# Sums and differences of mirrored samples ahead of the second transform stage, as 64 by 64 products, and a new plan for the front

## The chip, the cores and the metric

The kernel runs on one core of a Trainium2 chip. The metric is the device time of one execution in microseconds; the kernel before takes 508.01 us, the median of three runs (507.02 to 508.63). The engines are named as in the profile: PE (TensorE), DVE (VectorE), ACT (ScalarE), POOL (GpSimd), and SP, which here only issues DMAs. PE reads its operands from SBUF and writes PSUM.

## The reference

For a sequence of L = 2048 tokens with D = 512 channels, the output is a gated sum of two branches of the same input x:

```python
g = sigmoid((x * gate_w).sum(-1, keepdims=True))
K = einsum("dn,dnl,dn->dl", Cc, exp(dt * A * l), dB).real          # taps: 512 channels, 2048 long, 128 states
a = irfft(rfft(pad(x)) * rfft(pad(K)))[:L] + x * Dskip            # causal convolution along the sequence
b = gelu(x @ w1 + b1) @ w2 + b2                                   # dense branch, 512 -> 1792 -> 512
out = g * a + (1 - g) * b
```

## The kernel before, in words

The program has two parts. **The front** (`front`) does the whole dense branch but its last bits, makes the taps K, and runs the first transform stage of the signal and of the taps. **The tail** (`conv`) does the second stage of both transforms, their product, the two inverse stages, the gate and the output.

A transform of 2048 samples is split as 32 times 64. The first stage (`first_stage`, L438) multiplies 32-row slices by c1t, a 32 by 64 matrix (32 complex frequencies), and its result goes through DRAM (`tu_d` for the signal, `tk_d` for the taps) so that the 64 remaining samples of each of the 32 frequencies come to lie on partitions: 128 rows are 64 real and 64 imaginary parts. The second stage (`pair`, L1152, called from `taps` and `signal` in the tail) turns these 128 rows into 64 real and 64 imaginary results for each frequency: one product of all 128 rows by a 128 by 64 matrix for the real part, one by another for the imaginary part. Of the second matrix only the first is loaded (c2); `matrices` makes it from the loaded one by a swap of halves and a sign, on POOL for the first two groups of four frequencies, on ACT for the other six. A step s of the tail takes two frequencies: `product` multiplies the two spectra on DVE in six operations (L1174 to L1179), `inverse` (L1191) does the first inverse stage in 64 by 64 products, and `turn` sends the result through DRAM (`t_d`) to the final stage (L1316). PE's order within a step is signal(s+1), taps(s+2), inverse(s). Nine leftover products of the dense branch stand before the inverse of the last step and the others behind it (`rest`).

The order of all work in the front is set by a planner (`Plan`). Each piece of work has an engine, a cost, a due time and the buffers that it reads and writes; the planner lets each engine take the ready piece with the lowest due time, and the program is then written in that order, fixed for each engine. The due times come from some fifty numbers at the head of the file (T_0, K_0, U_0, D_S1 and so on). In the front each block of 256 tokens goes through `hidden` (L917 to L919: three float32r products for each 128 by 128 tile of w1), gelu on ACT, a subtraction on DVE (L947) and `output` (L962 to L964). The taps come in 16 groups: DVE builds powers (L532 to L535), magnitudes (L689) and rotations (L701 to L712), PE contracts them (`contract`, L726), DVE adds the skip term (L743), ACT copies the result to SBUF (L744, tile s), and after every second group a first stage runs; ACT copies its four results into `sk` (L752), and after four groups SP stores them to `tk_d` (L767).

POOL in the front only clears buffers (L678) and issues DMAs: the reloads of x (L848) and the additions into the output in DRAM (L992, L1006). The signal's slots lie in the order of `slot_q`, which puts mirrored samples q and 63 - q into slots 32 apart.

Of the kernel before, what the change touches and what calls it, by code (L numbers as in the profile page):

```python
# [17 lines left out]
P = 128  # L18
L = 2048
D = 512  # L20
# [12 lines left out]
NB = 2 * NSB  # L33
T_0 = 28.031
T_MLP = 402.005
K_0 = 34.529
T_KG = 347.257
U_0 = 23
U_GAP = 18
LAG = 13.166  # L40
TABLE = 30.571
D_KA = -21.02
D_KP = -70.174
D_S1 = -64.005
D_EV = -0.687
D_H = -44.182
D_LO = -26.872
PS = (2, 3, 1, 2)
N_ACC, N_H, N_PK, N_PU = PS
D_SP = -0.459  # L50
MEM = (6, 2, 3)
N_LD, N_HL, N_ST = MEM
D_XS = -150.061
D_G = 2.936
N_WARM = 13
T_EARLY, T_LOFT, T_DEN = 434.731, 499.385, 583.061
Y_K, Y_U = 40.448, 33.741
W_MLP = (-0.0424, -0.0295, 0.0137)
W_KG = (-0.0358, -0.0266, -0.0229)
W_U = (-0.0255, -0.1355, -0.0209)  # L60
D_MAG = -1.089
D_ROT = 0.621
D_CON = -2.254
D_PHA = 0.57
D_PRE = -1.138
D_XL = 26
D_COE = -4.808
D_OUT = -10.383
D_DTB = -996.723
D_D0A = -269.982  # L70
D_LAST = -1.103
N_REST = 3
D_KA0 = 35
D_DT = 5
D_PRM = -94
D_D0 = 0
D_WAVE0 = -333.922
D_COE0 = -195.511
D_SP1 = -346.272
D_G0 = 14  # L80
D_GW = 568.694
D_XS0 = 115.71
T_PRE = 23
W_CAST = (0, 1, 0, 0, 1, 0, 1, 0, 1, 1, 0, 1, 0, 0)
X_CAST = (1, 1, 1, 1)
D_X0, D_B2, D_B2A, D_DM = -480, 20, -11.213, -79.268
N_G = 9
# [44 lines left out]
def constants():  # L132
# [7 lines left out]
    p = np.arange(32)  # L140
    q = np.asarray(slot_q())
    k1 = np.arange(64)
# [3 lines left out]

    c1 = np.tile(np.stack([er, ei], 2).reshape(32, 64), (4, 1))

# [21 lines left out]

    f2 = np.zeros((32, 2, 64, 64))
    g2 = np.zeros((32, 64, 32, 2))
    for n, k in enumerate(ko):
        er, ei = om(4 * np.outer(q - 31.5, k + 32 * k1) + (q - 31.5)[:, None])
        f2[n, 0], f2[n, 1] = er, -ei
        a = 2.0 * np.pi * (k + 32 * k1 + 0.25) / L
        g2[n, :, :, 0] = np.cos(np.outer(a, m))
        g2[n, :, :, 1] = np.sin(np.outer(a, m))
        g2[n, :, 0, 1] = 1 - 2 * (k1 % 2)
# [131 lines left out]
def gated_mix(  # L311
# [33 lines left out]
    gate = cp.tile([P, 2, 16], F32, name="gate")  # L345
    c1t = cp.tile([P, 64], F32, name="c1t")

# [5 lines left out]
    def front(pool, psum, keep, attic, loft, den):  # L353
# [45 lines left out]
        ux = [rooms[0], *tiles(1, [P, D], "ux")]  # L399
        s1 = tiles(2, [P, D], "s1")  # L400

        xh, xlo = (
# [24 lines left out]

        def first_stage(xs, due, evac, ahead=2):

            q = (step[0] + ahead) % N_H  # L430
            banks = [(phs[q].rearrange("p a b -> p (a b)"), ("h", q)), (pks[0].rearrange("p g s -> p (g s)"), ("pk", 0))]
            banks += [(pus[k], ("pu", k)) for k in range(2)]

            def products():
                for r, (bank, _) in enumerate(banks):
                    rs = slice(32 * r, 32 * r + 32)
                    for m, (x, _) in enumerate(xs):
                        nc.tensor.matmul(bank[64 * m : 64 * m + 64], c1t[rs], x[rs], start=True, stop=True)  # L438
# [7 lines left out]
        def signal():  # L446
            for s in range(8):
                t = U_0 + 16 * U_GAP * warp(s / 8, W_U)
                yield t + Y_U
                xs = [(ux[m], ("ux", m)) for m in range(2)]  # L450
                for m in range(2):
                    move(256, lambda m=m, s=s: nc.sync.dma_start(ux[m], xl[2 * s + m]), t - 10, [], [("ux", m)])

                def evac(r, pp, key, s=s, t=t):
                    k = take("st", N_ST)
                    act(512, lambda: nc.scalar.copy(st[k], pp), t + D_EV, [key], [("st", k)])
                    for m in range(2):
                        move(
                            128, lambda m=m: nc.sync.dma_start(rows[:, 8 * s + 4 * m + r], st[k][64 * m : 64 * m + 64]),
                            t, [("st", k)], [("u_d", 8 * s + 4 * m + r)], out=True,  # L460
                        )

                first_stage(xs, t, evac)
            yield None
# [251 lines left out]
        def contract(u, c, k, t):  # L716
# [27 lines left out]
            act(512, lambda: nc.scalar.copy(xs, pks[q].rearrange("p s g -> p (s g)")), t + D_S1, [("pk", q)], [key])  # L744
            pair.append((xs, key))
            if c % 2 == 0:
# [11 lines left out]

            first_stage([pair.pop(0), pair.pop(0)], t, evac, 1 if g == 4 * NCH - 1 else 2)
            if c < NCH - 1:  # L760
# [349 lines left out]
    def conv(pool, ps, late, attic, loft, den):  # L1110
# [5 lines left out]
        ko = k0_order()  # L1116
        c4s, mats, t2s = {}, {}, {}

        def consts(m):
            cc = pool.tile([P, 384], F32, tag="cc", name=f"cc{m}", bufs=4)  # L1120
            nc.sync.dma_start(cc, c2[m])
            c4s[m] = cc

# [6 lines left out]

        def matrices(m):

            cc = c4s[m]
            f = cc[:, 0:256].rearrange("p (n k) -> p n k", n=4)
            f1 = pool.tile([P, 4, 64], F32, tag="f1", name=f"f1{m}", bufs=2)
            if m < 2:
                nc.gpsimd.tensor_scalar(f1[0:64], f[64:128], -1.0, None, ALU.mult)
                nc.gpsimd.tensor_copy(f1[64:128], f[0:64])
            else:
                nc.scalar.mul(f1[0:64], f[64:128], -1.0)  # L1140
                nc.scalar.copy(f1[64:128], f[0:64])
            mats[m] = (f, f1), cc[:, 256:384].rearrange("p (s k) -> p s k", s=2)

        fac, pus, prod, pas = {}, {}, {}, {}

        def pair(s, r, c, out):

            for i in range(2):
                n = 2 * s + i
                w = mats[n // 4][0][c][:, n % 4]  # L1150
                x = t2s[n] if r else us[n]
                nc.tensor.matmul(out[64 * i : 64 * i + 64], w, x, start=True, stop=True)  # L1152

        def taps(s):
            fac[s] = []
            for c in range(2):
                pk = ps.tile([P, D], F32, tag=f"pk{c}", name=f"p2k{s}{c}", bufs=1)
                pair(s, 1, c, pk)
                k = pool.tile([P, D], F32, tag=f"k{c}", name=f"k{s}{c}", bufs=2)
                nc.scalar.copy(k, pk)  # L1160
                fac[s].append(k)

        def signal(s):
            pus[s] = []
            for c in range(2):
                pu = ps.tile([P, D], F32, tag=f"pu{2 * (s % 2) + c}", name=f"p2u{s}{c}", bufs=1)
                pair(s, 0, c, pu)
                pus[s].append(pu)

# [87 lines left out]
        nc.sync.dma_start(g1t, g1.rearrange("p (b k) -> p b k", b=2))  # L1257
        matrices(0)
        matrices(1)
        taps(0)  # L1260
        signal(0)
        taps(1)
        for s in range(16):
# [22 lines left out]
            turn(s)  # L1286
            if s % 2 and s < 13:
                matrices(s // 2 + 2)
            if 7 <= s < 13:
# [132 lines left out]
```

## Time and profile before

| | |
|---|---|
| median of three runs | 508.01 us |
| profiled execution, span | 506.3 us (no other time of that execution is given; the median is 1.7 us above the span) |
| PE, DVE, ACT, POOL busy | 494.8, 429.0, 347.2, 53.5 us |
| front, to the first product of the second stage | 398.2 us |
| 16 steps of the tail, to the last inverse product | 398.2 to 476.6 us |
| leftover dense products, then final stage and output | 476.6 to 487.0, 487.0 to 506.3 us |

A float32 product shows as two records, so a row "x8" on L1152 or L1191 is four products. Durations of PE records overlap; the spacing of their starts, or the merged pieces of the chain of waits, tells what a product costs. In the views by stretch, each engine's busy time stands with its number of instructions in brackets, then the granted clock, the busy share of the 16 DMA engines and GB/s; the DMA share can pass 1.

### The profile page before, as it was taken

To read this page: it belongs to the slowest core of one execution; us is meant where nothing else is said; L and a number is where in the kernel's file an instruction comes from. 1 tells how busy PE (TensorE), PEld (TensorE's weight loads), DVE (VectorE), ACT (ScalarE), POOL (GpSimd) and SP (SyncE) were. 2 spreads that over 40 slices of the span, in tenths; PEclk is the share of its full clock that TensorE was granted. 3 is DMA by queue.
4 is the path that set the end of the run, shared out by engine and by line. 5 is a ranking of instruction groups with operands and counts; after the bars stand their busy time and mean duration, and the time that the engine had idled before them with its cause. 6 is when DMAs were issued, how large, how long until landed. Compare 5 with 4: busy or idle time off the path is not lost.

```text
span 506.3 us, 12185 instructions
## 1 busy us (share of the span) xinstructions
PE 494.8 (98%) x4798; PEld 380.3 (75%) x4798; DVE 429.0 (85%) x794; ACT 347.2 (69%) x625; POOL 53.5 (11%) x93
## 2 busy tenths in 40 slices
PE   7999999999999999999999999999999999999995
PEld 7886988998889889889789878989889722222551
DVE  6999999998999999999899989999921188877544
ACT  4898757699683889968487997657643445568513
POOL 1001010101002011011110012001010300020003
PEclk9999999999999999999999999999999999999998
DMA  8958896416788545889850276984588997999998
GB/s 288 381 178 235 298 296 219 84 65 200 182 239 222 156 147 126 262 187 238 201 128 2 84 167 156 208 266 104 189 208 180 282 390 266 336 374 382 320 321 312
DMA packets 82680, 112.32 MB, mean 222 GB/s; under 512 B 39644, under 2 KB 41184, under 8 KB 82080
## 3 DMA queue, kind: packets, MB, share of 16 engines
q1 hardware_dynamic: 74704, 87.06, 53.7%
q0 software_dynamic: 7264, 21.73, 18.3%
q10 hardware_dynamic: 656, 2.75, 1.7%
q8 instruction: 38, 0.62, 0.5%
q14 instruction: 18, 0.15, 0.1%
HBM read 61.71 MB, written 49.81 MB: 220 GB/s over the span
## 4 chain that ended last, share of the span: by engine, by line
PE 70%; DVE 13%; DMA 7%; ACT 4%; SPq 2%; issue 2%; DVEq 0%; ACTq 0%
PE pk L726 10%; PE acc L962 7%; PE ph L917 7%; PE ph L919 7%; PE ph L918 7%; PE acc L964 7%; PE acc L963 6%; PE p2u L1152 5%; PE p2k L1152 4%; PE pa L1191 3%; PE pb L1316 3%; DMA tk<-tk_d 2%; PE ph L438 2%; DVE y L689 2%; SPq L767 2%
## 5 line engine op out<-in xcount | busy, mean ns | idle before, releaser
L917 PE MATMUL ph<-xh,wh 128*128 128x256 f32 x448 | 127.7, 285 | 2.2 <-ACT wh L826 1.6
L919 PE MATMUL ph<-xh,wl 128*128 128x256 f32 x448 | 127.1, 284 | 0.4 <-DVE wl L828 0.4
L918 PE MATMUL ph<-xlo,wh 128*128 128x256 f32 x448 | 126.7, 283 | 0.0
L917 PEld LDWEIGHTS ph<-xh,wh 128*128 128x128 f32 x448 | 85.2, 190 | 9.5 <-issue 5.0
L918 PEld LDWEIGHTS ph<-xlo,wh 128*128 128x128 f32 x448 | 85.1, 190 | 1.8
L919 PEld LDWEIGHTS ph<-xh,wl 128*128 128x128 f32 x448 | 85.1, 190 | 1.0 <-DVE wl L828 1.0
L962 PE MATMUL acc<-wh,hh 128*128 128x512 f32 x206 | 83.2, 404 | 0.1
L964 PE MATMUL acc<-wh,hl 128*128 128x512 f32 x206 | 80.9, 393 | 0.5 <-DVE hl L947 0.5
L963 PE MATMUL acc<-wl,hh 128*128 128x512 f32 x206 | 80.9, 393 | 0.0
L934 ACT ACTIVATE ph<-ph,b1t 128x256 f32<-128x256 f32 x112 | 50.4, 450 | 43.6 <-PE ph L919 41.8
L726 PE MATMUL pk<-y,den 128*32 128x64 f32 x2048 | 61.4, 290 | 0.0
L726 PEld LDWEIGHTS pk<-y,den 128*32 128x32 f32 x2048 | 57.2, 136 | 3.5 <-issue 1.4
L962 PEld LDWEIGHTS acc<-wh,hh 128*128 128x128 f32 x206 | 38.7, 188 | 17.8 <-issue 7.4
L947 DVE TENSOR_TENSOR hl<-ph,hh 128x512 fp32r<-128x512 f32 (+1 forms) x62 | 38.4, 620 | 14.9 <-ACT hh L937 14.6
L689 DVE TENSOR_TENSOR y<-y,ea 128x64 f32<-128x64 f32 (+4 forms) x80 | 45.5, 569 | 2.1 <-ACT y L679 1.5
L964 PEld LDWEIGHTS acc<-wh,hl 128*128 128x128 f32 x206 | 38.7, 188 | 10.3 <-DVE hl L947 1.7
L963 PEld LDWEIGHTS acc<-wl,hh 128*128 128x128 f32 x206 | 38.7, 188 | 6.2
L937 ACT CAST hh<-ph 128x512 fp32r<-128x512 f32 (+1 forms) x62 | 33.0, 533 | 9.4 <-PE acc L963 6.2
L532 DVE TENSOR_TENSOR loft<-den,zz 128x256 f32<-128x256 f32 (+2 forms) x48 | 37.4, 779 | 0.7
L533 DVE TENSOR_TENSOR loft<-den,zz 128x256 f32<-128x256 f32 (+2 forms) x48 | 37.3, 777 | 0.0
L701 DVE TENSOR_TENSOR y<-y,loft 128x2048 f32<-128x2048 f32 x16 | 36.6, 2288 | 0.6 <-ACT loft L650 0.5
L1160 ACT COPY k<-p2k 128x512 f32<-128x512 f32 x32 | 18.5, 585 | 23.8 <-PE p2k L1152 8.0
(190 smaller groups left out, 876.0 us busy)
## 6 DMA issues: line engine op xcount, KB each, us to landing
tu_d<-attic SPq DMA_DIRECT2D x64, 128.0 KB, 3.9
tk_d<-sk SPq DMA_DIRECT2D x32, 256.0 KB, 5.3
t_d<-sa SPq DMA_DIRECT2D x32, 256.0 KB, 5.4
tk<-tk_d SPq DMA_DIRECT2D x24, 256.0 KB, 5.1
attic<-in_xt_dram SPq DMA_DIRECT2D x16, 256.0 KB, 5.1
xh_d<-xh SPq DMA_DIRECT2D x8, 512.0 KB, 5.0
xl_d<-xlo SPq DMA_DIRECT2D x8, 512.0 KB, 4.6
attic<-in_xs_dram SPq DMA_DIRECT2D x16, 256.0 KB, 4.9
```

Of the source, the lines that this page charges most:

```text
L532: vec(2 * m, lambda: vv.tensor_mul(t, a, br), due, [ka, *kb], [kt])
L689: nc.vector.tensor_mul(both(n, 64 - 3 * n, n), both(0, 64 - n, n), an)
L726: nc.tensor.matmul(pks[q][32 * j : 32 * j + 32, :, gg], x[:, r, :, ch], y[:, r, :, ch], start=(r == 0), stop=(r == 1), skip_group_check=True,)
L917: nc.tensor.matmul(p, h, xh[xk][:, d], start=(d == 0), stop=False)
L918: nc.tensor.matmul(p, h, xlo[xk][:, d], start=False, stop=False)
L919: nc.tensor.matmul(p, lo, xh[xk][:, d], start=False, stop=(d == 3))
L934: nc.scalar.activation(phs[q][:, n], phs[q][:, n], AF.Gelu_apprx_tanh, bias=b1t[:, f : f + 1])
L947: nc.vector.tensor_sub(lo, phs[q][:, 0:nf], hi.bitcast(F32))
L962: nc.tensor.matmul(a, h, wh[1][w], start=start, stop=False)
L963: nc.tensor.matmul(a, h, wl[1][w], start=False, stop=False)
L964: nc.tensor.matmul(a, l, wh[1][w], start=False, stop=(j == 3))
L1152: nc.tensor.matmul(out[64 * i : 64 * i + 64], w, x, start=True, stop=True)
```

## The change

For a real input at a real transform, the second stage on 64 slots needs only the sum of slots q and 63 - q for the cosine part and their difference for the sine part. The change makes these before the first stage. For the signal POOL subtracts and adds two loaded tiles of 512 columns (`ud`, `ux`), for which the two mirrored halves are now loaded together (`xl[s]` and `xl[s + 8]`); for the taps POOL subtracts and adds the halves of each copied contraction, 256 columns each (`sd`, and in place in `s1`). c1t gets a second matrix for the differences, so that what comes out of the first stage has 64 rows for the real result and 64 rows for the imaginary one. The taps' first stage works on half as many columns in twice as many products. In the tail each of the two results then needs 64 rows by a 64 by 64 matrix, and all matrices are loaded: `matrices` is gone. POOL's scratch for DMA descriptors is set to 8192 bytes, which makes room for the new tiles, and nearly all of the planner's numbers are others.

```diff
-T_0 = 28.031
+T_0 = 26.408
...
+D_UD = -20.4
...
+        def pool_op(n, fn, due, reads=(), writes=()):
+
+            return pl.add("GP", 0.18 + n / 470.0, fn, due, reads, writes)
...
-                    for m, (x, _) in enumerate(xs):
-                        nc.tensor.matmul(bank[64 * m : 64 * m + 64], c1t[rs], x[rs], start=True, stop=True)
-
-            mm(1.04, products, due + D_S1, [*(key for _, key in xs), "c1"], [key for _, key in banks], 0.5, 1.06, "f32")
+                    for m, parts in enumerate(xs):
+                        ms = slice(64 * m, 64 * m + 64)
+                        for x, at, sign in parts:
+                            c = c1t[rs, 64 * sign : 64 * sign + 64]
+                            nc.tensor.matmul(bank[ms, at], c, x[rs], start=True, stop=True)
+
+            mm(hold, products, due + D_S1, [*keys, "c1"], [key for _, key in banks], 0.5, 1.06, "f32")
...
-                    move(256, lambda m=m, s=s: nc.sync.dma_start(ux[m], xl[2 * s + m]), t - 10, [], [("ux", m)])
+                    move(256, lambda m=m, s=s: nc.sync.dma_start(ux[m], xl[s + 8 * m]), t - 10, [], [("ux", m)])
+                pool_op(512, lambda: nc.gpsimd.tensor_sub(ud, ux[0], ux[1]), t + D_UD, [("ux", 0), ("ux", 1)], ["ud"])
+                pool_op(512, lambda: nc.gpsimd.tensor_add(ux[0], ux[0], ux[1]), t + D_UD, [("ux", 1)], [("ux", 0)])
...
-            pair.append((xs, key))
+            low, high, df = xs[:, 0 : D // 2], xs[:, D // 2 : D], sd[c % 2]
+            pool_op(256, lambda: nc.gpsimd.tensor_sub(df, low, high), t + D_S1, [key], [("sd", c % 2)])
+            pool_op(256, lambda: nc.gpsimd.tensor_add(low, low, high), t + D_S1, [], [key])
+            pair.append([(low, slice(0, D // 2), 0), (df, slice(D // 2, D), 1)])
...
-        def matrices(m):
-
-            cc = c4s[m]
-            f = cc[:, 0:256].rearrange("p (n k) -> p n k", n=4)
-            f1 = pool.tile([P, 4, 64], F32, tag="f1", name=f"f1{m}", bufs=2)
-            if m < 2:
-                nc.gpsimd.tensor_scalar(f1[0:64], f[64:128], -1.0, None, ALU.mult)
-                nc.gpsimd.tensor_copy(f1[64:128], f[0:64])
-            else:
-                nc.scalar.mul(f1[0:64], f[64:128], -1.0)
-                nc.scalar.copy(f1[64:128], f[0:64])
...
-        def pair(s, r, c, out):
-
-            for i in range(2):
-                n = 2 * s + i
-                w = mats[n // 4][0][c][:, n % 4]
-                x = t2s[n] if r else us[n]
-                nc.tensor.matmul(out[64 * i : 64 * i + 64], w, x, start=True, stop=True)
+        def pair(s, r, outs):
+
+            for c in range(2):
+                rows = slice(64 * c, 64 * c + 64)
+                for i in range(2):
+                    n = 2 * s + i
+                    w = mats[n // 4][0][rows, n % 4]
+                    x = (t2s[n] if r else us[n])[rows]
+                    nc.tensor.matmul(outs[c][64 * i : 64 * i + 64], w, x, start=True, stop=True)
...
-    nc = bacc.Bacc("TRN2", target_bir_lowering=False, num_devices=1)
+    nc = bacc.Bacc("TRN2", target_bir_lowering=False, num_devices=1, dynamic_dma_scratch_size=8192)
```

Three places of the new order matter for what follows. The lines of the changed file stand lower by 10 to 20: L448 is the first stage, L462, L463, L759 and L760 are POOL's new operations, L691 clears, L867, L1011 and L1025 are POOL's DMAs, L786 the store of the taps, L494 the early load of the signal, L1151 the load of the taps, L1163 the second stage, L1201 the inverse.

The first is PE in one step of the tail, before and after. cc is a tile of loaded matrices, f one made by `matrices`; p2u and p2k are the results for signal and taps.

```order
L1191 MATMUL pa_4861<-v_4835,cc_4759 64x512
L1152 MATMUL p2u_4880<-den,cc_4767 64x512 x2
L1152 MATMUL p2u_4883<-den,f_4789 64x512 x2
L1152 MATMUL p2k_4886<-tk_4781,cc_4767 64x512
L1152 MATMUL p2k_4886<-tk_4783,cc_4767 64x512
L1152 MATMUL p2k_4891<-tk_4781,f_4789 64x512
L1152 MATMUL p2k_4891<-tk_4783,f_4789 64x512
L1191 MATMUL pa_4896<-v_4872,cc_4759 64x512
```

```order
L1201 MATMUL pa_5008<-v_4982,cc_4874 64x512
L1163 MATMUL p2u_5029<-den,cc_4882 64x512 x2
L1163 MATMUL p2u_5030<-den,cc_4882 64x512 x2
L1163 MATMUL p2k_5035<-tk_4927,cc_4888 64x512
L1163 MATMUL p2k_5035<-tk_4929,cc_4888 64x512
L1163 MATMUL p2k_5036<-tk_4927,cc_4888 64x512
L1163 MATMUL p2k_5036<-tk_4929,cc_4888 64x512
L1201 MATMUL pa_5045<-v_5021,cc_4882 64x512
```

The number of products and their order stay; the matrix f is gone, and each product takes 64 rows of tk or den instead of 128.

The second is POOL in the middle of the front, about where the reloads of x begin, before and after.

```order
L992 DMA out_dram<-b2b 128x512 x4
L678 MEMSET y 128x32
L848 DMA xh_105<-xh_d 128x1024
L848 DMA xlo_107<-xl_d 128x1024
L678 MEMSET y 128x32
L992 DMA out_dram<-b2b 128x512
```

```order
L1011 DMA out_dram<-b2b 128x512 x2
L691 MEMSET y 128x32
L759 TENSOR_TENSOR sd_106<-s_104 128x256
L760 TENSOR_TENSOR s_104<-s_104 128x256
L867 DMA xh_108<-xh_d 128x1024
L867 DMA xlo_110<-xl_d 128x1024
L691 MEMSET y 128x32
L759 TENSOR_TENSOR sd_105<-s_103 128x256
L760 TENSOR_TENSOR s_103<-s_103 128x256
L867 DMA xh_109<-xh_d 128x1024
L867 DMA xlo_111<-xl_d 128x1024
L1011 DMA out_dram<-b2b 128x512 x2
```

POOL's reads of SBUF now stand between its DMAs, one pair for each of the 16 groups of taps; the pairs for the signal (L462, L463) stand at eight other places.

The third is SP at the hand-over from front to tail, before and after: the last store of the taps, early loads of the signal, and the first loads of the tail.

```order
L481 DMA den<-tu_d 128x512
L767 DMA tk_d<-sk 64x16x64 x8
L481 DMA loft<-tu_d 128x512
L481 DMA den<-tu_d 128x512 x2
L1121 DMA cc_4759<-in_c_dram 128x384
L1129 DMA tk_4761<-tk_d 128x512
```

```order
L494 DMA den<-tu_d 128x512
L786 DMA tk_d<-sk 64x16x64 x8
L494 DMA den<-tu_d 128x512
L1140 DMA cc_4874<-in_c_dram 128x384
L1151 DMA tk_4876<-tk_d 128x512
```

Two early loads have moved ahead of the last store. On PE, 24 instead of 12 dense products of the hidden layer (L917 to L919) stand between the last contraction and the last first stage of the taps, and 96 instead of 120 behind that stage, beside 30 of the output layer in both.

More of the change, by code (lines that the diff above doesn't have):

```diff
@@ L140, in constants @@
     p = np.arange(32)
-    q = np.asarray(slot_q())
     k1 = np.arange(64)
@@ L400, in front @@
         s1 = tiles(2, [P, D], "s1")
+        sd = tiles(2, [P, D // 2], "sd")
+        ud = pool.tile([P, D], F32, name="ud")
         xh, xlo = (
@@ L1163, in signal @@
         def signal(s):
[L1164 to L1168, printed above, removed]
+            pus[s] = [
+                ps.tile([P, D], F32, tag=f"pu{2 * (s % 2) + c}", name=f"p2u{s}{c}", bufs=1) for c in range(2)
+            ]
+            pair(s, 0, pus[s])
         def product(s):
```

129 lines of the change are left out of this document (66 added, 63 removed).

## The prediction

> **What bounds the kernel now.** I read the page first, then the busy times by stretch, then the chain of waits in the tail, then VectorE's own order of time there.
>
> ```profile
> span 506.3 us, 12185 instructions
> PE 494.8 (98%) x4798; PEld 380.3 (75%) x4798; DVE 429.0 (85%) x794; ACT 347.2 (69%) x625; POOL 53.5 (11%) x93
> ```
>
> ```profile
> 25.00:350.00 325.00, 322.77 (x3625) 279.30 (x3624) 314.70 (x599) 252.25 (x447) 33.61 (x57) 1.00 0.67 181
> ...
> 408.00:420.00 12.00, 11.09 (x58) 3.12 (x60) 12.00 (x21) 6.53 (x13) 0.00 (x0) 1.00 1.02 374
> ...
> 424.00:436.00 12.00, 12.00 (x64) 3.45 (x62) 9.24 (x17) 7.29 (x15) 1.69 (x3) 1.00 0.81 253
> 436.00:452.00 16.00, 16.00 (x88) 4.20 (x84) 13.25 (x23) 8.73 (x16) 1.44 (x3) 1.00 1.01 380
> 452.00:472.00 20.00, 20.00 (x108) 5.50 (x104) 15.39 (x26) 15.70 (x29) 2.23 (x5) 1.00 1.02 378
> ```
>
> In the front two engines are full at once: of 325 us PE is busy 322.8 and DVE 314.7, so DVE has only 10.3 us to spare. POOL, which gets the new work, has nearly all its time free. In the tail PE is full and DVE, once it has caught up (408 to 420), is not.
>
> ```profile
> 418.78 1.02 PE pa L1191 x8
> 419.80 1.87 PE p2u L1152 x8
> 421.67 1.72 PE p2k L1152 x8
> 423.38 1.02 PE pa L1191 x8
> ```
>
> This is one step of the tail on the chain: 1.02 + 1.87 + 1.72 = 4.61 us, all PE. Four products of 64 by 64 (L1191) take 1.02 us where four of 128 by 64 (L1152) take 1.72 to 1.87. DVE in the same loop, in order of time:
>
> ```profile
> 406.37 0.69 DVE L1175 TENSOR_TENSOR v<-p2u,k 128x512 f32<-128x512 f32 x1 [1.95 <-DMA out_dram<-io]
> ...
> 409.37 0.69 DVE L1174 TENSOR_TENSOR v<-p2u,k 128x512 f32<-128x512 f32 x1
> ...
> 412.96 0.69 DVE L1174 TENSOR_TENSOR v<-p2u,k 128x512 f32<-128x512 f32 x1
> ...
> 453.15 0.69 DVE L1174 TENSOR_TENSOR v<-p2u,k 128x512 f32<-128x512 f32 x1 [0.92 <-ACT sa L1197]
> ...
> 457.75 0.69 DVE L1174 TENSOR_TENSOR v<-p2u,k 128x512 f32<-128x512 f32 x1 [0.92 <-ACT sa L1197]
> ...
> 474.59 0.69 DVE L1179 TENSOR_TENSOR v<-v,z 128x512 f32<-128x512 f32 x1
> ```
>
> Where its inputs are ready, six operations take 412.96 - 409.37 = 3.59 us; later a step takes 4.60, with 0.92 idle ahead of each.
>
> **The tail's loop.** With both second-stage sets in the form of L1191, PE needs 3 x 1.02 = 3.06 us a step, and DVE with 3.59 becomes the slowest. The sixteen DVE sets now run from 405.8 (406.37 less the first operation) to 475.2, 69.4 us; at 3.59 they take 57.4. That is the upper bound, 12.0 us saved. ACT does not stand in the way: two copies of each kind and, in the last six steps, two scalings.
>
> ```profile
> L1160 ACT COPY k<-p2k 128x512 f32<-128x512 f32 x32 | 18.5, 585 | 23.8 <-PE p2k L1152 8.0 <-issue 6.8 <-ACT f L1141 4.3
> L1197 ACT COPY sa<-pa 128x512 f32<-128x512 f32 x32 | 17.2, 589 | 7.7 <-PE pa L1191 6.1 <-ACT loft L1234 1.6
> L1234 ACT ACTIVATE attic<-attic,gate 128x512 f32<-128x512 f32 x8 | 5.3, 720 | 0.0
> ```
>
> By the busy sums that is (18.5 + 17.2)/16 + 2 x 0.66 = 3.55 us in those steps, just under 3.59; so a little is lost there. What ACT did for f is gone, and hid behind PE anyway. The lower bound is from DMA. Its share is 1.01 to 1.02 from 436 to 472 at about 380 GB/s: nearly full. The five rows above and the 4 us between them (taken at the mean of their neighbours, 314) move 12 x 374 + 4 x 314 + 12 x 253 + 16 x 380 + 20 x 378 = 22.4 MB in 64 us; at 380 that is 59 us, 5 us saved. Part of these bytes is for the final stage and may land behind the loop, so I take 8, between the two.
>
> **The end keeps its length.** Behind the last inverse product come leftover dense products and then the final stage:
>
> ```profile
> 475.60 1.02 PE pa L1191 x8
> ...
> 487.04 13.91 PE pb L1316 x68
> ```
>
> The 10.4 us between are PE's own work over the last store and reload of t_d; both move forward together with the loop's end. Cost 0; without that cover the DMAs alone would set the start of L1316, at the same place within a us or two.
>
> **The front's new products.** Each first stage of the taps has twice as many products on half the columns, so the same columns in all. Eight such stages; one takes 203.59 - 202.54 = 1.05 us now. What a small product costs PE is bounded by the contraction, 128 records in 3.8 us, 0.03 us each: 16 more records are 0.5 us a stage and 4 us for the eight. The other bound is 0, if eight tiles still run side by side and only columns count. I take 1 us, nearer to 0, since in L1152 against L1191 it is columns and tiles that decide.
>
> ```profile
> 202.54 0.64 PE L438 MATMUL ph<-attic,c1t 32*64 32x512 f32 x1
> ...
> 203.59 0.50 PE L962 MATMUL acc<-wh,hh 128*128 128x512 f32 x1
> ...
> 60.14 3.76 PE pk L726 x121
> ```
>
> **The hand-over.** The last taps go from the copy of the contraction over the first stage, four copies into sk, eight stores and the first loads to the first product of the tail:
>
> ```profile
> 374.40 0.59 ACT L744 COPY s<-pk 128x512 f32<-128x512 f32 x1 [4.86 <-DVE pk L743]
> ...
> 375.68 0.13 PEld L438 LDWEIGHTS ph<-s,c1t 32*64 32x64 f32 x2
> ...
> 377.34 1.97 ACT sk L752 x4
> 379.32 0.61 SPq L767
> ...
> 388.00 5.11 DMA tk_d<-sk
> ...
> 388.87 1.37 SPq L481 DMA_DIRECT2D loft<-tu_d  x1
> 390.33 1.67 SPq L481 DMA_DIRECT2D den<-tu_d  x2
> ...
> 393.19 0.32 SPq L1129
> ...
> 398.24 1.34 PE L1152 MATMUL p2k<-tk,cc 128*64 128x512 f32 x4
> ...
> 374.56 0.12 PE ph L919
> ```
>
> POOL's two operations enter between L744 and L438. POOL's price is between the 0.18 us of one column and the 1.27 us of 512 columns with two inputs:
>
> ```profile
> L1330 POOL TENSOR_TENSOR loft<-loft,sa 128x512 f32<-128x512 f32 x2 | 2.5, 1271 | 22.9 <-DMA t<-t_d 22.5 <-ACT sa L1329 0.4
> ...
> L1014 POOL COPY look<-xh 128x1 f32<-128x1 f32 x1 | 0.2, 184 | 24.7 <-ACT xh L937 24.7
> ```
>
> For 256 columns I take the middle, 0.73, so 1.5 us a pair. The new order has 12 more dense products ahead of that first stage, 12 x 0.12 = 1.4 us, which cover it almost exactly; there is no slack. Counted back from the tail, 24 dense products fewer stand behind the stage, 2.9 us, so the first loads would come late by as much, but two early loads (some 1.67 us of SP's queue) have gone from between, and the first load waited for the landing of the last store anyway (388.00 + 5.11). That leaves up to 2 us on PE ahead of the tail's first product; DVE's second operation waited until 406.37 for another DMA, so I book 0 of it (bounds 0 and 2).
>
> Sum: -8 for the loop, +1 for the split products, 0 for hand-over and end, -7 us. On the profiled execution: 506.3 to 499.3; the median stands 1.7 above that span, so 508.0 to **501 us**. Own range, from -12 to -5 and +0 to +6 for the other two: 496 to 505 (the upper ends don't come together).
>
> **Rival one: POOL holds up DVE in the front (slower).** POOL now does 16 operations of 1.27 us and 32 of 0.73, 43.7 us, all reading SBUF while DVE works without a gap. In the trace POOL in the front only clears and issues DMAs, so nothing shows what the two do to each other. If a POOL operation keeps DVE from its next one, DVE falls behind, its results come late to contractions that PE reaches in fixed order, and PE waits. DVE operations that read PSUM and one SBUF tile are taken as free of this:
>
> ```profile
> L689 DVE TENSOR_TENSOR y<-y,ea 128x64 f32<-128x64 f32 (+4 forms) x75 | 42.7, 569 | 2.1 <-ACT y L679 1.5
> ...
> L701 DVE TENSOR_TENSOR y<-y,loft 128x2048 f32<-128x2048 f32 x15 | 34.3, 2289 | 0.6 <-ACT loft L650 0.5
> L947 DVE TENSOR_TENSOR hl<-ph,hh 128x512 fp32r<-128x512 f32 (+1 forms) x50 | 31.0, 619 | 2.0 <-ACT hh L937 1.7
> ```
>
> The last row is theirs, 31.0 of 314.7 us, a tenth; 0.9 x 43.7 = 39 us would hit DVE if held for whole lengths, less 10.3 us to spare, 29 us; with -7 that gives 530. At three quarters of the lengths 29 - 10 - 7 = +12: 520 us, the time of this rival. It decides from 17 us of hold-up, 44% of the lengths. The other bound is 0. For it speaks that DVE is 97% full and that POOL reads SBUF throughout; against it that no row shows such a wait. The Trainium skill, page SBUF — State Buffer, section "Who interferes with whom", states it as a rule: a DVE instruction with two SBUF inputs contends with a GpSimd instruction that reads SBUF, and whichever comes second is blocked until the first ends. No run here shows it. By that rule in full the time would be the 530 above, and without it the forecast.
>
> **Rival two: DMA paces the loop.** The share of 1.02 speaks for it; 253 GB/s from 424 to 436, where there is room, against it. Saved are 5 instead of 8 us, and about half a us more goes at the end where stores queue: 504.5 us.
>
> **Rival three: no change.** POOL's pair has no slack ahead of PE's first stage. If each of eight waits one DVE operation more (0.6 us) plus a late clear or DMA issue on POOL's queue, 0.9 us each, 7 us go on PE, and 508 results. The same follows if the 64 by 64 products do not run four at a time; L1191 speaks against that.
>
> **Chances.** Forecast 0.45, rival one 0.35, two 0.10, three 0.10. A measurement here tells about 0.3% from no change, 1.5 us. Faster by more: forecast and rival two, 0.55; within: 0.09; slower: rival one and a little of three, 0.36. The range, 495 to 523 us, takes in the forecast's own and most of rival one, leaving out its upper part.
>
> **What would show it.** Right: chain steps of L1163 and L1201 with 1.02 us each, DVE in the tail without 0.92 idle and about 3.6 to 3.8 us a step, 25 to 350 with PE near 322 of 325. Rival one: DVE operations of the same form longer than before (L701 over 2.29, L689 over 0.57) or gaps put down to POOL, PE idle on DVE in the front, and the first L1163 well behind 400. Rival two: a DMA share over 1 with idle on ACT or PE for tk. Rival three: idle ahead of L448 put down to L759 or L760. The forecast is wrong if the first product of the tail comes later than about 406, whatever the tail then saves.

## The result, and the profile after

The changed kernel takes 524.2 us, the median of four runs (523.5 to 529.5), against 507.8 for the kernel before on the same chip (507.0 to 508.6, four runs): a ratio of 1.035, 95% interval 1.030 to 1.041. The forecast was 501 us and rival one's time 520. What came is rival one, and a little more of it.

From the page, two groups of DVE's operations before, then the busy times and the same two groups of the changed kernel:

```profile
L689 DVE TENSOR_TENSOR y<-y,ea 128x64 f32<-128x64 f32 (+4 forms) x80 | 45.5, 569 | 2.1 <-ACT y L679 1.5
...
L532 DVE TENSOR_TENSOR loft<-den,zz 128x256 f32<-128x256 f32 (+2 forms) x48 | 37.4, 779 | 0.7
```

```profile
PE 487.1 (93%) x4926; PEld 387.2 (74%) x4926; DVE 455.3 (87%) x794; ACT 344.3 (66%) x616; POOL 113.9 (22%) x137
...
L702 DVE TENSOR_TENSOR y<-y,ea 128x64 f32<-128x64 f32 (+4 forms) x80 | 54.9, 686 | 0.4
...
L545 DVE TENSOR_TENSOR loft<-den,zz 128x256 f32<-128x256 f32 (+2 forms) x48 | 42.1, 878 | 0.8 <-ACT den L671 0.3
```

DVE has the same 794 instructions as before and is busy for 455.3 us instead of 429.0: 26.3 us more for the same work. That is a net figure: the forms that nothing holds up are a little shorter in this execution (0.681 us for 0.689 in L966), so the hold-up itself is somewhat larger. The busy times by stretch of the changed kernel (the middle of the front, then a stretch of the tail's loop):

```profile
25.00:350.00 325.00, 310.68 (x3470) 266.45 (x3470) 318.49 (x567) 242.96 (x427) 81.31 (x91) 0.99 0.63 167
436.00:452.00 16.00, 15.15 (x112) 5.55 (x109) 16.00 (x28) 9.82 (x19) 0.97 (x2) 1.00 1.04 389
```

In the front DVE is a little busier than before (318.5 against 314.7), but in the same 325 us it finishes 567 instructions where it finished 599, and PE stands still for 14.3 us where it stood still for 2.2. In the tail's loop the roles are as forecast: DVE is full, PE no longer.

| | before | after |
|---|---|---|
| last rotation of DVE in the front starts | 367.1 | 391.6 |
| first product of the tail's second stage | 398.2 | 422.0 |
| last inverse product ends | 476.6 | 492.2 |
| final stage starts | 487.0 | 502.6 |
| span | 506.3 | 521.5 |

So the front loses 23.8 us, the loop wins 78.4 - 70.2 = 8.2, the end stays. The last rotations, from DVE in order of time, of before and then of the changed kernel, show that the loss is complete before the hand-over begins:

```profile
367.07 1.22 DVE L712 TENSOR_TENSOR y<-y,loft 128x1024 f32<-128x1024 f32 x1
```

```profile
391.64 1.22 DVE L725 TENSOR_TENSOR y<-y,loft 128x1024 f32<-128x1024 f32 x1
```

**Where DVE's time went.** POOL's four new groups in the changed kernel, and then one form of DVE's operations with both inputs in SBUF and the one that reads PSUM, before and after, from the views that keep shapes apart:

```profile
L760 POOL TENSOR_TENSOR s<-s 128x256 f32<-128x256 f32 x16 | 20.0, 1252 | 0.9
L759 POOL TENSOR_TENSOR sd<-s 128x256 f32<-128x256 f32 x16 | 16.7, 1044 | 38.3 <-ACT s L757 38.3
L462 POOL TENSOR_TENSOR ud<-attic,ux 128x512 f32<-128x512 f32 x8 | 14.6, 1824 | 53.9 <-DMA attic<-in_xl_dram 30.7 <-issue 12.4 <-DMA ux<-in_xl_dram 10.7
L463 POOL TENSOR_TENSOR attic<-attic,ux 128x512 f32<-128x512 f32 x8 | 12.8, 1595 | 0.5
```

```profile
L947 DVE TENSOR_TENSOR hl<-ph,hh 128x512 fp32r<-128x512 f32 x46 | 31.7, 689 | 13.3 <-ACT hh L937 13.2
...
L532 DVE TENSOR_TENSOR loft<-den,zz 128x256 f32<-128x256 f32 x16 | 6.8, 424 | 0.3
```

```profile
L966 DVE TENSOR_TENSOR hl<-ph,hh 128x512 fp32r<-128x512 f32 x46 | 31.3, 681 | 13.5 <-ACT hh L956 13.5
...
L545 DVE TENSOR_TENSOR loft<-den,zz 128x256 f32<-128x256 f32 x16 | 9.4, 586 | 0.3 <-ACT den L671 0.3
```

POOL's operations take 64.1 us in all where their shortest examples (0.73 us for 256 columns, 1.29 for 512) add up to 44. DVE's operation on two SBUF tiles goes from 0.42 to 0.59 us on the mean; the one that reads ph from PSUM doesn't grow (0.69, then 0.68). Two moments of the changed kernel, DVE and then POOL in order of time, show both sides of one wait. In the first the two engines take turns:

```profile
62.94 0.68 DVE L548 TENSOR_TENSOR den<-loft 128x512 f32<-128x512 f32 x1
63.66 1.40 DVE L545 TENSOR_TENSOR loft<-den,zz 128x256 f32<-128x256 f32 x1
64.98 1.52 DVE L546 TENSOR_TENSOR loft<-den,zz 128x256 f32<-128x256 f32 x1
```

```profile
63.03 1.75 POOL L462 TENSOR_TENSOR ud<-attic,ux 128x512 f32<-128x512 f32 x1 [8.52 <-DMA attic<-in_xl_dram]
64.86 1.36 POOL L463 TENSOR_TENSOR attic<-attic,ux 128x512 f32<-128x512 f32 x1
```

POOL's L462 begins beside DVE's L548 and gets 0.46 us longer; DVE's next two, 0.42 us each by themselves, take 1.40 and 1.52 and end 0.28 us behind POOL's two. In the second, POOL waits through a row of such DVE operations:

```profile
81.22 1.21 DVE L721 SCALAR_TENSOR_TENSOR y<-y,loft 128x1024 f32<-128x1024 f32 x1
...
83.69 0.28 DVE L548 TENSOR_TENSOR den<-loft 128x128 f32<-128x128 f32 x1
83.89 0.41 DVE L966 TENSOR_TENSOR hl<-ph,hh 128x256 fp32r<-128x256 f32 x1
84.22 1.45 DVE L545 TENSOR_TENSOR loft<-den,zz 128x512 f32<-128x512 f32 x1
```

```profile
82.03 3.10 POOL L462 TENSOR_TENSOR ud<-attic,ux 128x512 f32<-128x512 f32 x1 [7.64 <-DMA attic<-in_xl_dram]
```

L462 takes 3.10 us. Counted back from its end by its shortest length, 1.29, it gets going at about 83.8, when DVE turns to L966 (83.89), which has its first input in PSUM, and DVE's L545 then takes 1.45 instead of 0.69. PE pays at the products that need DVE's hl; from the waits up to 400 us, of before and of the changed kernel:

```profile
PE acc L964 <- DVE hl L947: 0.5, 1, 0.5
```

```profile
PE acc L983 <- DVE hl L966: 5.7, 6, 2.4
...
PE ph L448 <- POOL s L760: 1.6, 2, 1.1
```

All of PE's waits that are put down to hl come to 10.6 us up to 400, where they were 1.5. The granted clock fell too: it reads 0.93 from 25 to 50 and from 75 to 100 us, and 1.00 in both stretches of the run without reads below. What part of PE's loss that is was not separated.

**The theory** was then: POOL's reads of SBUF keep DVE's operations on two SBUF tiles from running, and the reverse, and that is all of the front's loss. Its rivals were POOL's writes, the new plan of the front or the smaller DMA scratch, PE's wait for POOL's pairs, tiles that POOL holds too long, and DVE's spare time swallowing a part.

### The profile page after: what moved, and what is told of

Read it like the earlier page. It is cut to its first block, busy times and chain, and to the rows that moved or that the text cites. A ratio compares the mean times of both kernels' runs of the same rounds, so it can differ in the third digit from the quotient of the medians.

```text
span 521.5 us, 12497 instructions
## 1 busy us (share of the span) xinstructions
PE 487.1 (93%) x4926; PEld 387.2 (74%) x4926; DVE 455.3 (87%) x794; ACT 344.3 (66%) x616; POOL 113.9 (22%) x137
## 5 line engine op out<-in xcount | busy, mean ns | idle before, releaser
L702 DVE TENSOR_TENSOR y<-y,ea 128x64 f32<-128x64 f32 (+4 forms) x80 | 54.9, 686 | 0.4
L966 DVE TENSOR_TENSOR hl<-ph,hh 128x512 fp32r<-128x512 f32 (+1 forms) x62 | 37.9, 612 | 19.2 <-ACT hh L956 19.1
L545 DVE TENSOR_TENSOR loft<-den,zz 128x256 f32<-128x256 f32 (+2 forms) x48 | 42.1, 878 | 0.8 <-ACT den L671 0.3
L546 DVE TENSOR_TENSOR loft<-den,zz 128x256 f32<-128x256 f32 (+2 forms) x48 | 41.3, 861 | 0.0
L1201 PE MATMUL pa<-v,cc 64*64 64x512 f32 x128 | 27.0, 637 | 9.7 <-ACT sa L1207 8.2
```

Of the source, the lines that this page charges most:

```text
L545: vec(2 * m, lambda: vv.tensor_mul(t, a, br), due, [ka, *kb], [kt])
L546: vec(2 * m, lambda: vv.tensor_mul(v, a, bi), due, [ka, *kb], [kv])
L702: nc.vector.tensor_mul(both(n, 64 - 3 * n, n), both(0, 64 - n, n), an)
L966: nc.vector.tensor_sub(lo, phs[q][:, 0:nf], hi.bitcast(F32))
```

## The experiments

Diffs are against the changed kernel or the kernel before, as named. Ratios are to the kernel before, run on the same chip in turn with each.

### POOL's operations without their reads, in the changed kernel

```diff
+        def twice(x):
+            for _ in range(2):
+                nc.gpsimd.memset(x, 0.0)
...
-                pool_op(512, lambda: nc.gpsimd.tensor_sub(ud, ux[0], ux[1]), ...)
+                pool_op(512, lambda: twice(ud), ...)
```

and so at the other three places.

> The changed kernel with POOL's 48 subtractions and additions replaced by clears of the same tiles, two clears for each, about as long (0.54 us for 512 columns, 0.32 for 256, by the clears of 32 and 128 columns in the trace). The data are zeros, so sums, differences and the result are left out; the order on PE, DVE, ACT and SP is the changed kernel's, row for row. Theory (POOL's reads of SBUF hold up DVE operations with two SBUF inputs): DVE's operations of one form fall back to the lengths of before (L702 from 0.69 to 0.57 us on the mean), the first product of the tail comes at 399 to 401 us instead of 422, the whole at about 500 to 502 us. Rival (the new plan's order, or the wait of PE for POOL's pair): stays at 518 to 524 us.

Measured: 503.8 us, ratio 0.994 (0.992 to 0.997). DVE is busy for 428.5 us, as before, and the tail's first product comes at 400.2; the time is 2 us above what the theory expected. From 25 to 350:

```profile
25.00:350.00 325.00, 322.38 (x3705) 281.16 (x3711) 312.40 (x597) 254.92 (x446) 65.25 (x141) 1.00 0.67 181
```

So with the same order on every engine 20 us go when the reads go. The new plan and the scratch are not the cause of these 20.

### POOL's reads, and POOL's writes, in the kernel before

To the kernel before are added 48 subtractions on POOL at the same places, into tiles that nobody reads; in a second kernel, 96 clears of the same tiles. The order of PE, DVE, ACT and SP is that of before. Both have the change's smaller scratch, which makes room for the tiles.

```diff
+                for _ in range(2):
+                    pool_op(512, lambda: nc.gpsimd.tensor_sub(ud, ux[0], ux[1]), ...)
...
+            for _ in range(2):
+                pool_op(256, lambda: nc.gpsimd.tensor_sub(df, low, high), ...)
```

> The kernel before with 48 more POOL operations in the front: for each of 8 signal stages two subtractions of 512 columns, for each of 16 tap groups two of 256, of the same tiles as in the change but into tiles that nobody reads. The result is the full one; the order on PE, DVE, ACT and SP is that of before, row for row. Theory (reads hold up DVE): slower by about what the front of the change lost, 15 to 24 us: 523 to 532 us, with L689 and L532 longer than 0.57 and 0.78 us. Rival (the new plan, or PE waiting for POOL's results): no change, 508 us.

> The kernel before with clears in place of the 48 operations of the run with reads, two clears for each, into the same tiles that nobody reads, with the same scratch for POOL's DMAs. Theory (it is the reads that hold up DVE): no change, 506 to 510 us. Rival (any work of POOL, its late DMAs, or the halved scratch costs the time): slower by several us, in the extreme as much as the run with reads.

Measured: 528.0 us with reads, ratio 1.041 (1.038 to 1.044); 506.8 with clears, ratio 0.999 (0.997 to 1.001). POOL's groups and DVE's busy time with the reads, then with the clears:

```profile
PE 504.1 (96%) x4798; PEld 382.7 (73%) x4798; DVE 460.0 (87%) x794; ACT 348.4 (66%) x625; POOL 116.5 (22%) x141
...
L755 POOL TENSOR_TENSOR sd<-s 128x256 f32<-128x256 f32 x32 | 35.0, 1093 | 26.2 <-ACT s L752 25.0
L460 POOL TENSOR_TENSOR ud<-attic,ux 128x512 f32<-128x512 f32 x16 | 29.1, 1820 | 62.9 <-DMA ux<-in_xl_dram 62.4
```

```profile
PE 494.6 (98%) x4798; PEld 379.5 (75%) x4798; DVE 429.6 (85%) x794; ACT 347.3 (69%) x625; POOL 89.9 (18%) x189
...
L374 POOL MEMSET sd<- 128x256 f32 x64 | 22.7, 355 | 2.7
L374 POOL MEMSET ud<- 128x512 f32 x32 | 18.8, 586 | 1.4
```

41.5 us of clears change nothing: DVE 429.6, the time within 0.2%. 48 subtractions whose results nobody uses stretch DVE by 31.0 us and cost 21. Up to the tail no wait of PE, ACT or DVE is put down to the added operations of the run with reads, so neither PE's wait for a pair nor a tile that POOL holds too long is the cause.

### The front of before with the new tail

```diff
-                x = t2s[n] if r else us[n]
-                nc.tensor.matmul(out[64 * i : 64 * i + 64], w, x, start=True, stop=True)
...
+                    x = (t2s[n] if r else us[n])[rows]
+                    nc.tensor.matmul(outs[c][64 * i : 64 * i + 64], w, x, start=True, stop=True)
```

with the products, copies and matrices of the changed tail, and nothing changed in the front.

> The kernel before with the tail of the change only: second stage in 64 by 64 products, no matrices made on ACT and POOL; the front is that of before, row for row on PE and DVE, so that the tail gets sums and differences that were never made and the result is not the reference's. Theory: the tail is worth what the change's tail shows, 8 us from its first product to the final stage: 499 to 501 us, with DVE at 3.6 us a step. Rival (DMA paces the tail as soon as it starts on time): 503 to 506 us.

Measured: 500.7 us, ratio 0.987 (0.984 to 0.990), 6 to 7 us less. That is the change's gain with its cost left out, and what the forecast foresaw for the whole. The rival, 503 to 506, fell.

### Half of the reads

In the changed kernel the taps' pairs only clear (first), or the signal's (second).

```diff
-            pool_op(256, lambda: nc.gpsimd.tensor_sub(df, low, high), ...)
+            pool_op(256, lambda: twice(df), ...)
```

> The changed kernel, its order of instructions unchanged; POOL's 16 subtractions and additions of the signal (512 columns, 20.3 us of POOL alone) stay, its 32 of the taps are clears (two each) that read nothing, so the taps' result is left out. With no reads at all the same program took 503.8, with all of them 524.2. Theory A, each hold-up passes on to PE by itself: the loss goes by POOL's reading time, 20.3 of 43.7 us, so 503.8 + 0.46 x 20.4 = 513. Theory B, DVE's spare time swallows the first part: DVE was stretched by 26 us with all reads, 12 of it here, about what it has to spare (12.6 us of 325 in the run without reads), so 504 to 508.

> The mirror of the run before: the signal's 16 operations are clears (its result left out), the taps' 32 operations of 256 columns (23.4 us of POOL alone) stay, each pair between the copy of a contraction and the first stage. Theory A: 503.8 + 0.54 x 20.4 = 515. Theory B: 14 us of stretch against 12.6 to spare, 505 to 509. If instead the taps' pairs cost because a first stage on PE waits for POOL, and not by DVE, this run holds nearly the whole loss (520 or more) and the one before nearly none.

Measured: 510.7 us, ratio 1.008 (1.005 to 1.010), with the signal's reads alone; 515.0, ratio 1.017 (1.014 to 1.020), with the taps'. Over the 503.8 without reads that is 6.9 and 11.1 us, together 18.0 of 20.4. Theory A gave 9 and 11, theory B at most 4 and 5. So A is nearer: DVE's spare time takes some of the first half and little of the second. DVE's busy time grows by 14.6 us with the signal's reads and by 12.6 with the taps', and yet the smaller stretch costs more. The view that keeps shapes apart tells whom each half meets; DVE with the signal's reads, then with the taps':

```profile
L549 DVE TENSOR_TENSOR loft<-den,zz 128x512 f32<-128x512 f32 x16 | 11.8, 736 | 0.3
...
L706 DVE TENSOR_TENSOR y<-y,ea 128x256 f32<-128x256 f32 x16 | 6.7, 418 | 0.1
```

```profile
L549 DVE TENSOR_TENSOR loft<-den,zz 128x512 f32<-128x512 f32 x16 | 11.0, 686 | 0.3
...
L706 DVE TENSOR_TENSOR y<-y,ea 128x256 f32<-128x256 f32 x16 | 9.4, 586 | 0.1
```

The signal's reads lengthen the powers (0.736 for 0.69) and leave the magnitudes alone; the taps' reads, which come behind each contraction, lengthen the magnitudes (0.586 for 0.42) and leave those powers alone. So the two halves stretch different operations, as they would if those grow that stand beside the reads.

### Reads with one input

The kernel before with POOL's 48 added subtractions made copies.

```diff
-                    pool_op(512, lambda: nc.gpsimd.tensor_sub(ud, ux[0], ux[1]), ...)
+                    pool_op(512, lambda: nc.gpsimd.tensor_copy(ud, ux[0]), ...)
```

> The kernel before, its own order kept, with POOL's 48 subtractions of the run with reads replaced by copies of one tile (one SBUF input in place of two) into the same tiles that nobody reads. Full result. If any POOL read of SBUF holds DVE up, by its length: a copy takes POOL between a clear (0.36 and 0.59 us) and a subtraction (0.73 and 1.27), so 25 to 44 us in all; at the loss per us of the subtractions (21 us for 43.7) that is 519 to 528, with the 128x256 powers near 0.5 us. Rival, only POOL operations with two inputs hold DVE up: 507, with the powers at 0.42.

Measured: 509.5 us, ratio 1.005 (1.003 to 1.007). Both expectations missed, the rival's by 2.5 us. POOL's groups and the busy times:

```profile
PE 497.3 (98%) x4798; PEld 380.3 (75%) x4798; DVE 439.9 (86%) x794; ACT 347.7 (68%) x625; POOL 93.1 (18%) x141
...
L755 POOL COPY sd<-s 128x256 f32<-128x256 f32 x32 | 25.0, 782 | 24.9 <-ACT s L752 24.0
L460 POOL COPY ud<-attic 128x512 f32<-128x512 f32 x16 | 16.7, 1044 | 56.6 <-DMA attic<-in_xl_dram 56.2
```

The copies do hold DVE up, by 10.9 us, and wait for it in turn (0.78 us on the mean, where the shortest pair takes 0.86, 0.43 each): so it isn't two inputs alone. Alone they would take some 25 us, the lower end of what was expected; for each us of that DVE is stretched by 0.44 us, where subtractions stretched it by 0.71. But the loss isn't in proportion: 10.9 us is about what DVE can spare, and little reaches the end. This is where DVE's spare time shows: 10.9 us of stretch cost 3 us here, 31.0 cost 21 with subtractions.

### All sums on DVE

```diff
-pool_op(512, lambda: nc.gpsimd.tensor_sub(ud, ux[0], ux[1]), ...)
+vec(512, lambda: nc.vector.tensor_sub(ud, ux[0], ux[1]), ...)
```

and the other three likewise.

> The changed kernel with all 48 subtractions and additions on DVE in place of POOL, full result; the planner sets them among DVE's other work. DVE gets 16 x 0.69 + 32 x 0.41 = 24 us at most (0.69 and 0.41 are the durations of its own operations of 512 and 256 columns without contention) on 312.4 busy us of 325, so 11 us too much: 503.8 + 11 = 515 if DVE's work is what counts. That is under 524, since contention stretched DVE by 26 us and made POOL late besides. Rival, that DVE's stretch is harmless and POOL's lateness made the loss: then DVE's spare time takes the 24 us nearly in full and 504 to 508 results. Rival, that it matters nothing who makes the sums: 524.

Measured: 514.1 us, ratio 1.015 (1.012 to 1.018), the number of the first theory, but partly by luck, since its sum doesn't come out that way. The 48 operations take 24.4 us by their records, but records of DVE that follow each other overlap (in the tail six of 0.68 us start within 3.60 us), and DVE's busy time grew by only 16.8 us over the 428.5 without reads. Less the 12.6 to spare that would be a loss of 4, where 10.2 came. Of the spare time only 5.8 us were used: DVE still stands idle for 6.8 of the 325 us, and 16.8 - 5.8 = 11 is about the loss. By the same measure POOL's making of the sums stretches DVE by 26.8 us (455.3): handing them to the idle engine was worse than not handing them over.

### Half of the change, with sums on DVE

Only the signal takes sums and differences, on DVE; the front has a plan of its own for it. In the first two kernels the taps' partitions are put in another order so that one loaded matrix serves both, for which each load of taps is split in two and the second matrix takes four copies instead of two operations; the second of them also gates two steps later. The diff shows the split load. The third keeps the taps' partitions and loads and loads the signal's matrices beside.

```diff
-            nc.sync.dma_start(t2s[n], tk_d[ko[n]])
+            for h in range(2):
+                nc.sync.dma_start(t2s[n][64 * h : 64 * h + 64], tk_d[h, ko[n]])
```

> The kernel before with one half of the change: only the signal uses sums and differences, made by DVE (16 operations of 512 columns), and the front planned for that; the taps keep their 128 by 64 products, with their partitions in the order half, then component, so that one loaded matrix serves both. Full result. No POOL operation reads SBUF in the front. Theory: DVE's forms keep their lengths (the 128x256 powers 0.42 and not 0.58 us); 16 x 0.69 = 11 us of DVE work stand against 10.3 to spare, so 1 to 4 us are lost in the front; in the tail PE needs 1.02 + 1.72 + 1.02 = 3.76 us a step, about what DVE needs (3.6), so 5 to 6 us are won, as in the run of the old front with the new tail (-7.1). Sum 503 to 507 against 507.8. Rival: the tail's gain needs both transforms in the new form; then 508 to 511.

> The run before, and ACT's gating of the output rows (L1244 of the changed kernel) two steps later in the loop, so that the copies of k and sa behind it on ACT do not wait for a load from DRAM. Full result. If that wait, 3.2 us on DVE in the changed kernel, is a cost by itself: 2 to 3 us under the run before. Rival: the loop's DMA traffic is the limit and the same bytes come as late: within 1 us of it.

> The half change again (only the signal on sums and differences, made by DVE), with the taps' partitions and loads as in the kernel before (24 loads of 256 KB where the run before had 48 of 128 KB), and the signal's matrices loaded beside the taps' (c2 of 640 columns in place of 384, 1 MB more). Full result, the same plan of the front. The half change with split loads had a front as fast as before (PE 322.4 of 325 us) and lost all in the tail, where PE waited for tk loads and SP's queue held twice as many of them. If the split loads are the cause, the tail steps fall to 3.8 us: 503 to 507. Rival, DVE's sums or the half change itself cost it: 515 or more.

Measured: 523.4 us, ratio 1.031 (1.028 to 1.034); 522.4, 1.029 (1.026 to 1.032); 506.9, 0.999 (0.997 to 1.001). The busy times of the first by stretch (front, then tail), and what PE waited for in the tail:

```profile
25.00:350.00 325.00, 322.44 (x3604) 278.87 (x3603) 316.56 (x605) 252.95 (x448) 33.77 (x57) 1.00 0.69 182
...
424.00:436.00 12.00, 8.63 (x47) 2.49 (x48) 8.44 (x14) 5.61 (x11) 0.00 (x0) 0.87 0.79 246
```

```profile
PE p2k L1160 <- ACT f L1149: 10.1, 5, 6.2
PE p2k L1160 <- DMA tk<-tk_d: 8.0, 3, 4.4
```

My expectation for the first missed by 16 us at least. DVE's forms keep their lengths (0.42 us for the 128x256 powers), and up to 350 us PE is as full as before (322.4 of 325), but the last rotation comes at 372.8 instead of 367.1 and the tail's first product at 404.2 instead of 398.2: some 6 us are lost up to there, 4.4 of them in one wait of PE for a load of taps. The rest is my own edit of the tail, whose loop takes 85.8 us instead of 78.4: PE waits for the halved loads and for the four copies. The later gating brings 1 us at most. With both edits undone (the third) the loop takes 71.0 us, most of its steps 3.6 to 4.1; which of the two weighed more wasn't separated. But there too the first tail product comes at 403.9, 4.3 us of that in one wait for a load of taps, the stretch from the last inverse product to the final stage is 2 us longer, and so nothing is left over. No complete kernel that was run is faster than the kernel before.

### The gating two steps later in the changed kernel

```diff
-            if s > 9:
-                gated(HERE[s - 10])
+            if s > 11:
+                gated(HERE[s - 12])
```

The last two gatings come behind the loop. The occasion was a stall late in the changed kernel's loop, ACT and then DVE in order of time:

```profile
481.93 1.33 ACT L1244 ACTIVATE attic<-attic,gate 128x512 f32<-128x512 f32 x2 [5.25 <-DMA attic<-out_dram]
```

```profile
483.76 0.69 DVE L1184 TENSOR_TENSOR v<-p2u,k 128x512 f32<-128x512 f32 x1 [3.19 <-ACT k L1171]
```

> The changed kernel with ACT's gating two steps later and nothing else. Full result. If the wait of ACT for the load (5.25 us on ACT, 3.19 on DVE) is a cost by itself: 524.2 - 3 = 521. Rival, DMA is the limit of the loop's end: 523 to 524.

Measured: 526.5 us, ratio 1.038 (1.035 to 1.041): no gain. ACT's waits from 425 to 500 us, in the changed kernel and in this one:

```profile
ACT sa L1207 <- DMA t_d<-sa: 6.0, 3, 3.6
ACT attic L1244 <- DMA attic<-out_dram: 5.2, 1, 5.2
```

```profile
ACT sa L1207 <- DMA t_d<-sa: 11.8, 3, 5.7
```

The wait has gone from the load to the stores of t_d, and the loop takes 70.8 us where it took 70.2. So moving this one instruction doesn't help: the DMAs hold the loop's end up, whichever instruction meets them. They are not all of it, since PE's clock falls behind each of the two stalls (last section).

## Why the prediction was wrong, point by point

- **The hold-up of DVE by POOL, booked at nothing, is the step that failed.** The prediction had the mechanism as rival one and gave it 0.35, with "no row shows such a wait" against it. Three runs show it: reads gone, 504; reads added to the kernel before, 528; writes added, 507. DVE was stretched by 26.3 us, 60% of the 43.7 us that POOL's operations take alone; rival one was to decide from 17 us (its 44% are of the 39 us that it let fall on DVE, and of those 26.3 are 67%). Of the signs named for rival one, the late first product (422.0) and the longer L689 came; L701 kept its 2.28 us, since in the changed kernel hardly any of POOL's new operations ran beside it (0.06 us in all). In the run with copies one did, and it took 2.69. The Trainium skill, page SBUF — State Buffer, section "Who interferes with whom", states it so: a DVE operation on two SBUF inputs and a GpSimd operation that reads SBUF exclude each other, one that only writes does not disturb. The runs agree in each part: 460.0 us of DVE with reads, 429.6 with writes, 0.68 us for the form that reads PSUM. It should have had the larger chance.
- **The price of rival one**: 39 us for full lengths, less 10.3 to spare. Full lengths were too much, since POOL also waits for DVE and runs beside the operations that read PSUM. The rule "stretch less spare time" was too kind: with 26.3 us it gives a loss of 16, and 20 came; with the signal's reads alone 14.6 - 10.3 = 4, and 7 came. What it misses is that only a part of the spare time gets used. DVE is idle for 12.6 of the 325 us without reads and still for 6.5 with all of them. Stretch over the 428.5 without reads, less the idle time that went, gives 26.8 - 6.1 = 20.7 (20.3 came), 14.6 - 5.6 = 9.0 for the signal's reads (6.9 came) and 12.6 - 3.1 = 9.5 for the taps' (11.1 came). Why the rest of the spare time could not be used was not tested.
- **The tail's loop, -8**: 8.2 in the profiled executions. DVE sets the step where its inputs are there (440.56 to 444.16, 3.60 us); the end is held up by the DMAs, as the lower bound had it, and by some 3 us of slower clock, which the prediction did not have (last section). The run with the old front and the new tail gives 6 to 7 for the whole. In that sense rival two was a part of the forecast rather than another way.

```profile
440.56 0.68 DVE L1184 TENSOR_TENSOR v<-p2u,k 128x512 f32<-128x512 f32 x1
...
444.16 0.68 DVE L1184 TENSOR_TENSOR v<-p2u,k 128x512 f32<-128x512 f32 x1
```

- **The split first-stage products, +1, and the hand-over, 0**: right, and the first a little too large. Counted from the starts of PE's records, a first stage of the taps takes 1.10 us in seven of eight cases without reads, where it took 1.05: 0.4 us in all. From the start of the last rotation to the tail's first product it was 31.2 us before and is 30.4 now. With the reads gone, all the rest of the change comes to 503.8 - 500.7 = 3 us over the old front with the new tail; which part of the new front these are wasn't separated.
- **The end, 0**: 10.4 us from the last inverse product to the final stage, before and after.
- **Rival three** had its waits right and their effect wrong. In the changed kernel the eight first stages of the taps take 14.7 us where they took 8.4, and PE's waits put down to POOL stand in them. But the loss comes back whole where nobody waits for POOL's results, so these waits don't decide the time.

## What to carry to other kernels

An engine that is idle by its busy share is not free for work that reads SBUF while DVE is full: price each POOL operation with two SBUF inputs at five to seven tenths of its length on DVE (0.54 to 0.72 in four runs), a copy at about four (0.44 in one), don't count on all of DVE's spare time, and look for DVE operations of the same form that differ in length. Test such a price by adding the operation with an unused result to the kernel as it is; that takes a few lines and little else of the change (here the smaller scratch, for room). Where a gain of 6 us rests on some 24 us of new work elsewhere, ask first which engine really has that time.

## What the runs showed of the hardware that was not expected

- DVE operations that follow each other can keep a waiting POOL operation out through a whole row: L462 took 3.10 us where 1.29 is its shortest, an L759 2.84 and an L760 3.88 where 0.73 is, and each came in when DVE turned to L966, which reads PSUM. Elsewhere POOL came in behind a single one (L759 at 112.81 us took 0.86); what decides was not tested. Where POOL had started first, DVE waited to its end.
- A few DVE operations with one SBUF input were held up too: a conversion (L843) took 1.50 us at 20.43 beside L463, where the one before it took 0.42.
- POOL's copies with one input cost DVE a third of what subtractions of the same columns cost (10.9 against 31.0 us), though alone they take more than half as long (25 against 43.7).
- From 400 to 412 us the half change with split loads of taps (64 rows, 128 KB) moved 237 GB/s at a DMA share of 1.00, the one with whole loads 341 GB/s at 1.05. The two differ in other loads too, so the split is not shown to be the reason.
- After 4 us without a product (480 to 484 in the changed kernel) the granted clock was 0.50 for the next 4 us and 0.64 for the 4 behind them. That lies in the loop: from the last inverse but one to the last, with nine leftover products between, it is 491.11 - 484.76 = 6.35 us, where it was 475.53 - 472.23 = 3.30 at a clock of 1.00. So some 3 us of the loop's 70.2 are slower clock behind a stall:

```profile
480.00:484.00 4.00, 0.00 (x0) 0.00 (x0) 0.81 (x2) 2.07 (x4) 0.00 (x0) 1.00 0.97 382
484.00:488.00 4.00, 3.24 (x10) 1.34 (x11) 3.45 (x6) 3.57 (x8) 1.02 (x2) 0.50 1.06 408
```

```profile
484.76 2.46 PE L1201 MATMUL pa<-v,cc 64*64 64x512 f32 x8 [5.79 <-ACT sa L1207]
...
491.11 1.09 PE L1201 MATMUL pa<-v,cc 64*64 64x512 f32 x8
```
